# Moving a few small operations of routing and start-up between engines and steps

## The chip, the cores and the metric

One core of one Trainium2 chip runs the whole program. The metric is device time in microseconds (us), the median of the runs shown. The engines are named as the profile names them: PE (TensorE, matrix products) with PEld (its weight loads), DVE (VectorE), ACT (ScalarE), POOL (GpSimd) and SP (SyncE, which issues most of the DMAs).

## The reference

Attention in which a query sees only the keys of its own hash bucket, and behind it a layer of eight experts, each token going to the one with the highest logit:

```python
q_bits = (einsum('bhsd,dk->bhsk', q, proj) > 0)        # 6 bits, same for k
mask = q_bucket[:, :, :, None] == k_bucket[:, :, None, :]
scores = where(mask, scale * q @ k.T, -1e9)
attn = exp(scores - max(scores)); attn /= sum(attn) + 1e-9
x = (attn @ v) laid out as (B*S, H*D)                  # 3072 tokens x 512
logits = x @ w_gate                                    # 8 experts
expert = argmax(logits); weight = softmax(logits)[expert]
out[token] = weight * (relu(x @ w1[expert]) @ w2[expert])
```

There are 4 batches, 8 heads, 768 positions and 64 channels a head; w1 is 512 x 1024 and w2 1024 x 512 for each expert.

## The kernel before

The attention goes through 16 pairs of heads (pr = 0 to 15, four to a batch), each in two groups of 384 queries (g = 0, 1), each group in six steps (n = 0 to 5) of 128 queries of one head: 192 steps. The order of PE, DVE, ACT and SP is that in which the program is written; POOL's order is left to a scheduler, except for instructions wrapped in `in_turn`, which keep the written order among themselves.

A step i issues the scores of step i + 2 (`scores`: two products for each of two column ranges, L234 and L235), the row maximum on DVE (L237) and the exponential of step i + 1 on ACT (L253). Then come a small piece of other work, the transposes of probabilities (L278) and, in every second step, 24 products with v (L296). The codes of the buckets are carried as extra rows of the second operand of the scores.

At the start there is no pair before to hide behind. `first_k` and `first_q` make the operands of the two heads of pair 0: a rounded part (q1, k1) by ACT or DVE, the rest by a subtraction (L200 on DVE for head 0 and on POOL for head 1, L226 on POOL for q of both heads), and the codes (L205, L227, weighed by L210). The first scores need all of these for head 0. Two copies that only the routing of tokens needs, the triangle `tri` and the start of the counts `run` (L548, L549), are issued on POOL in front of them in the program.

A batch is routed in two groups. The pieces of `route` are put on a list, `light`, from which a step takes one: the logits, their gathering, the one-hot choice, `ranks` (PE counts the tokens of each expert in front of a token, into a PSUM tile `rk` of the pool `ps_m`, which has one buffer named `misc`), and `rows` (slot and weight of each token, and the scatter of its row to DRAM by POOL, L395). `av_out` transposes finished outputs into another tile of the same one buffer (L326) and scales them (L327). For the first group of a batch `rows` takes the next piece of the list in the same step, and that is `av_out` of the second group.

After the third batch `pick_first` chooses the expert that is computed first (L607 to L620): the fullest one by the counts so far. Its weights and rows are fetched during the last pairs, its first products (L729) run while the last rows are still scattered, and the eight experts follow.

`early_logits` (L502 to L517) sums three of the four pairs of the last group ahead of its end, in the last group's steps 0 and 1. `last_route` treats the last 384 tokens in three chains of 128; its first piece, `evac`, copies the output out of PSUM (L432).

Of the kernel before, what the change touches and what calls it, by code (L numbers as in the profile page):

```python
# [8 lines left out]
F32 = mybir.dt.float32  # L9
# [4 lines left out]
ALU = mybir.AluOpType  # L14
AX = mybir.AxisListType
# [3 lines left out]
P = 128  # L19
# [5 lines left out]
E, F = 8, 1024  # L25
# [33 lines left out]
def lsh_attention_moe_kernel(ctx, tc, qkd, q2d, k2d, v, pjbd, wg, w1, w2, ident_in, tri_in, cols_in, eoff_in, ids_in, out):  # L59
# [21 lines left out]
    tri = const.tile([P, P], BF16, name="tri")  # L81
    ones = const.tile([P, P], BF16, name="ones")
    V.memset(ones, 1.0)
    tiny = const.tile([P, 1], F32, name="tiny")
    V.memset(tiny, 1e-9)
    run = const.tile([P, E], F32, name="run")

    att = ExitStack()
# [38 lines left out]
    def in_turn(ins):  # L127
        if not in_turn_over:
            tc.keep_in_program_order(ins)
# [203 lines left out]
    def route(b, g):  # L333
# [19 lines left out]
        at = {}  # L353
# [22 lines left out]
        def ranks():  # L376
            A.activation(ex, lg, AF.Exp, bias=0.0, scale=1.0)
            rk = ps_m.tile([P, 512], F32, name="misc")
            PE.matmul(out=rk[:, 0:3 * E], lhsT=ident, rhs=run.unsqueeze(1).broadcast_to([P, 3, E]), start=True, stop=False)
            PE.matmul(out=rk[:, 0:3 * E], lhsT=tri, rhs=ohb, start=False, stop=False)  # L380
            PE.matmul(out=rk[:, E:3 * E], lhsT=ones, rhs=ohb[:, 0:2], start=False, stop=False)
            PE.matmul(out=rk[:, 2 * E:3 * E], lhsT=ones, rhs=ohb[:, 0], start=False, stop=True)
            for jj in range(3):
                PE.matmul(out=rk[:, 3 * E:4 * E], lhsT=ones, rhs=ohb[:, jj], start=jj == 0, stop=jj == 2)
            V.tensor_tensor(out=pos, in0=rk[:, 0:3 * E].rearrange("p (j e) -> p j e", e=E), in1=ohb, op=ALU.mult)
            V.tensor_tensor(out=run, in0=rk[:, 3 * E:4 * E], in1=run, op=ALU.add)
            V.reduce_sum(out=mx[:, :, 1:2], in_=ex, axis=AX.X)

        def rows():
            x = xrows[(b, g)]  # L390
            V.reduce_max(out=slot, in_=pos, axis=AX.X)
            V.tensor_tensor(out=mx[:, :, 1:2], in0=mx[:, :, 1:2], in1=tiny.unsqueeze(1).broadcast_to([P, 3, 1]), op=ALU.add)
            V.reciprocal(out=x[:, :, :, SEG + 1], in_=mx[:, :, 1:2].broadcast_to([P, 3, NG]))
            for jj in range(3):
                ins = G.indirect_dma_start(out=xs, out_offset=bass.IndirectOffsetOnAxis(ap=slot[:, jj, :], axis=0),  # L395
                                           in_=x[:, jj].rearrange("p g w -> p (g w)"), in_offset=None)
                rows_apart("xs", ins)
                if jj == 0 and b + 1 < B:
                    in_turn(ins)
            if not g and b + 1 < B:  # L400
                light.pop(0)()

        def pause():
            pass

        return [logits, gather_heads, one_hot, pause, ranks, rows] if b + 1 < B else [logits, gather_heads, one_hot, ranks, rows]

    def last_route(sums, o):
# [9 lines left out]
        def chain(jj, pools):  # L418
# [10 lines left out]
                return cell["t"]  # L429

            def evac():
                V.tensor_copy(out=ot, in_=o[:, js])  # L432
                G.tensor_scalar(out=sums[:, 2 * jj:2 * jj + 2], in0=sums[:, 2 * jj:2 * jj + 2], scalar1=1e-9, scalar2=None, op0=ALU.add)
                V.reciprocal(out=inv[:, jj], in_=sums[:, 2 * jj:2 * jj + 2])

# [109 lines left out]
    SY.dma_start(out=lsb[:, 0:P], in_=tri_in)  # L545
    SY.dma_start(out=eoff, in_=eoff_in)
    SY.dma_start(out=ids, in_=ids_in)
    G.tensor_copy(out=tri, in_=lsb[:, 0:P])  # L548
    G.tensor_copy(out=run, in_=eoff[:, 1])  # L549
    for hh in range(2):  # L550
        q1, k1 = (opp.tile([P, S], F32R, name=n) for n in ("q1", "k1"))
        operands[0][0][hh] += [q1, seconds(0)[:, 2 * hh], k1, seconds(0)[:, 2 * hh + 1]]
# [52 lines left out]
    def keys():  # L605

        V.tensor_tensor(out=key, in0=run, in1=eoff[:, 1], op=ALU.subtract)  # L607
        V.scalar_tensor_tensor(out=key, in0=key, scalar=float(2 * E), in1=eoff[:, 0], op0=ALU.mult, op1=ALU.add)

    def pick_first():  # L610

        def most():
            keys()
            V.reduce_max(out=best[:, 0:1], in_=key, axis=AX.X)

        def which():
            V.tensor_scalar(out=mark[:, 0], in0=key, scalar1=best[:, 0:1], scalar2=None, op0=ALU.is_equal)
            V.tensor_tensor(out=mark[:, 1], in0=mark[:, 0], in1=eoff[:, 0], op=ALU.mult)
            V.reduce_sum(out=best[:, 1:2], in_=mark[:, 1], axis=AX.X)
            V.tensor_scalar(out=best_i, in0=best[:, 1:2], scalar1=-1.0, scalar2=float(E), op0=ALU.mult, op1=ALU.add)  # L620

        return [most, which]

    def number(tile_1):
        return nc.values_load(tile_1, engines=[SY.engine], min_val=0, max_val=E - 1, skip_runtime_bounds_check_because=why)
# [115 lines left out]
    def out_and_route(pr, g):  # L741
        while divide:
            divide.pop(0)()
        if pr % NPAIR < NPAIR - 1:
            av_out(pr, g)
            return

        pieces = route(pr // NPAIR, g)
        pieces[0]()
        light.append(lambda: av_out(pr, g))  # L750
        light.extend(pieces[1:])
        if (pr, g) == (NPR - NPAIR - 1, 1):
            light.extend(pick_first())

    in_order.enter_context(tc.manual_schedule(engines={PE.engine, V.engine, A.engine, SY.engine}))
    put, weigh = first_k(0, V)
# [13 lines left out]
    for i, (pr, g, jj, hh) in enumerate(steps):  # L770
# [37 lines left out]
            run_expo(i + 1)  # L808
        if i == 0:
            weigh()  # L810
        while late:
            late.pop(0)()
        sums = sums_of(pr, g)
# [3 lines left out]
        side = (g, n) == (0, 2) and 0 < pr < NPR - 1  # L817
        if due and due[0][0] == i and not last:
            due.pop(0)[1]()
        elif light and not side and not last:  # L820
            light.pop(0)()
        if not last:
            for f, x in PREPARE[min(pr, 1)].get((g, n), ()) if pr + 1 < NPR else ():
# [19 lines left out]
            prev = (pr, g, sums)  # L843

        if last:
            if n < 2 and light:
                light.pop(0)()
            if n == 1:
                due.pop(0)[1]()
                while light:  # L850
# [400 lines left out]
```

## Time and profile before

| what | value |
|---|---|
| median of 3 runs | 727.81 us (725.92 to 729.55) |
| the profiled execution | 725.06 us |
| its span in the trace | 722.8 us, so 2.26 us lie around it |
| PE busy | 694.4 us (96%) |
| PEld, DVE, ACT, POOL busy | 85%, 72%, 64%, 57% |

Matrix products are pipelined and overlap, so busy PE is not PE at its peak. A stretch in which PE is not busy is of more use here: it is time in which it had nothing that could start. Attention ends at about 440 us; behind that PE is busy for the whole of nearly every stretch.

### The profile page before, as it was taken

The numbers are of one execution on the slowest core, as the hardware profiler recorded it, in microseconds if no ns is written. First come the engines' busy times: TensorE is split into PE (matmuls) and PEld (weight loads), VectorE is DVE, ScalarE is ACT, GpSimd is POOL, SyncE is SP. The second block draws the span as 40 slices with busy tenths as digits, with TensorE's granted clock in tenths as the row PEclk, the third lists the DMA queues.
The fourth block names the chain that finished last, engine by engine and source line by source line (L and its number), as shares of the span: only waits on it lengthen the run. The fifth ranks groups of instructions, "written<-read, shape, count | busy, mean of one in ns | idle before, by whom it ended". The sixth has DMA issues, their size and how long they took to land.

```text
span 722.8 us, 16061 instructions
## 1 busy us (share of the span) xinstructions
PE 694.4 (96%) x5735; PEld 612.1 (85%) x5735; DVE 517.1 (72%) x1018; ACT 463.8 (64%) x995; POOL 410.6 (57%) x405
## 2 busy tenths in 40 slices
PE   3999999999999999999989999999999999999995
PEld 1688888888887788887868879999999999999994
DVE  3857887888888988888998867656565657575641
ACT  3879888888888888897777853524242434354330
POOL 2577664776766586566766523018383838446461
PEclk9999999999999999999999999999999999999998
DMA  8788888889888989997987423765746465757521
GB/s 278 211 245 247 250 266 260 244 258 308 264 251 246 279 248 280 284 271 207 290 260 196 142 58 109 198 169 145 185 130 195 128 194 163 201 167 222 156 70 46
DMA packets 110081, 150.33 MB, mean 208 GB/s; under 512 B 12548, under 2 KB 77990, under 8 KB 109992
## 3 DMA queue, kind: packets, MB, share of 16 engines
q1 hardware_dynamic: 105016, 136.52, 65.2%
q0 software_dynamic: 4976, 12.69, 4.9%
q8 instruction: 47, 0.77, 0.5%
q14 instruction: 42, 0.34, 0.1%
HBM read 94.23 MB, written 55.18 MB: 207 GB/s over the span
## 4 chain that ended last, share of the span: by engine, by line
issue 21%; POOL 14%; PE 11%; DVE 3%; DMA 3%; ACT 1%; SPq 1%; POOLq 1%; ACTq 0%; DVEq 0%
POOL y L1026 11%; PE o L296 4%; PE s L234 2%; PE t L278 2%; POOL yo L1024 2%; DMA y<-yo,tok 2%; PE s L235 1%; DVE m L237 1%; DMA xr<-xs 1%; ACT p L253 1%; PE s L729 1%; DMA xs<-xr,slot 0%; POOL tags L947 0%; PE misc L326 0%; POOL tags L943 0%
## 5 line engine op out<-in xcount | busy, mean ns | idle before, releaser
L237 DVE TENSOR_REDUCE m<-s 128x1 f32<-128x768 f32 x192 | 182.4, 950 | 56.3 <-PE s L235 41.3
L234 PE MATMUL s<-k,q 128*128 128x512 f32 (+1 forms) x384 | 149.2, 388 | 15.3 <-POOL q L226 7.4
L296 PE MATMUL o<-pt,vt 128*64 128x128 f32 x2304 | 146.8, 277 | 0.0
L296 PEld LDWEIGHTS o<-pt,vt 128*64 128x64 f32 x2304 | 123.8, 137 | 16.9 <-issue 10.8
L235 PE MATMUL s<-c 76*128 76x512 f32 (+1 forms) x384 | 123.6, 343 | 0.1
L253 ACT ACTIVATE p<-s,m 128x768 f32<-128x768 f32 x111 | 110.2, 993 | 16.2 <-DVE m L241 12.5
L281 ACT COPY pt<-t 128x384 f32<-128x384 f32 x222 | 95.6, 485 | 39.0 <-PE t L278 37.1
L1026 POOL DMA_INDIRECT y<-yo,tags x88 | 103.5, 1176 | 24.9 <-issue 22.6
L234 PEld LDWEIGHTS s<-k,q 128*128 128x128 f32 x384 | 73.2, 191 | 48.0 <-ACT pd L253 10.1
L278 PE MATMUL t<-ident,p 128*128 128x128 f32 x666 | 92.3, 274 | 0.0
L984 ACT ACTIVATE hh<-hps 128x352 fp32r<-128x352 f32 (+3 forms) x56 | 27.9, 499 | 96.8 <-PE hps L998 96.8
L698 DVE TENSOR_TENSOR wlo<-wraw,whi 128x1024 fp32r<-128x1024 f32 x60 | 73.3, 1223 | 18.2 <-ACT whi L693 18.2
L278 PEld LDWEIGHTS t<-ident,p 128*128 128x128 f32 x666 | 75.0, 140 | 11.0 <-issue 9.4
L253 ACT ACTIVATE pd<-s,m 128x768 f32<-128x768 f32 x81 | 80.2, 991 | 5.0 <-DVE m L241 0.7
L269 DVE STREAM_TRANSPOSE pt<-pq 128x768 f32<-128x768 f32 x81 | 78.4, 968 | 6.0 <-DMA pq<-moved 6.0
L235 PEld LDWEIGHTS s<-c 76*128 76x128 f32 x384 | 73.9, 193 | 9.0 <-ACT c L210 0.4
L1017 PE MATMUL hps<-hh,wlo 128*128 128x436 f32 (+6 forms) x224 | 75.8, 339 | 0.0
L1017 PE MATMUL hps<-hh,whi 128*128 128x448 f32 (+9 forms) x224 | 75.8, 338 | 0.0
L1017 PE MATMUL hps<-hl,whi 128*128 128x436 f32 (+6 forms) x224 | 75.7, 338 | 0.0
L998 PE MATMUL hps<-xh,whi 128*128 128x352 f32 (+3 forms) x224 | 75.3, 336 | 0.0
L998 PE MATMUL hps<-xl,whi 128*128 128x428 f32 (+6 forms) x224 | 74.9, 334 | 0.0
L998 PE MATMUL hps<-xh,wlo 128*128 128x428 f32 (+6 forms) x224 | 74.9, 334 | 0.0
(221 smaller groups left out, 1185.6 us busy)
## 6 DMA issues: line engine op xcount, KB each, us to landing
wraw<-w SPq DMA_DIRECT2D x64, 512.0 KB, 3.7
moved<-pd SPq DMA_DIRECT2D x324, 96.0 KB, 3.7
pq<-moved SPq DMA_DIRECT2D x81, 384.0 KB, 4.3
qk<-qkd SPq DMA_DIRECT2D x30, 384.0 KB, 8.7
xs<-zrow SPq DMA_DIRECT2D x8, 910.0 KB
vt<-v SPq DMA_DIRECT2D x16, 384.0 KB, 3.5
coded<-cr SPq DMA_DIRECT2D x15, 192.0 KB, 2.3
c<-coded SPq DMA_DIRECT2D x30, 72.0 KB
```

What stands on the lines that cost most here:

```text
L234: PE.matmul(out=s[:, c0:c1], lhsT=q1[:, qs], rhs=k1[:, c0:c1], start=True, stop=False)
L235: PE.matmul(out=s[:, c0:c1], lhsT=q2[0:KM, qs], rhs=k2[0:KM, c0:c1], start=False, stop=True)
L237: V.tensor_reduce(out=m[:, 0:1], in_=s[:, 0:S], axis=AX.X, op=ALU.max, negate=True)
L253: A.activation(to, of, AF.Exp, bias=m[:, 2:3], scale=m[:, 1:2], accum_out=sums[:, idx:idx + 1])
L269: V.transpose(out=pt()[:, hh].rearrange("p c (s j) -> p c s j", j=SQ), in_=q.rearrange("p s c i -> p c s i"))
L278: PE.transpose(out=t[:, i * P:i * P + P], in_=p[:, kc * P:kc * P + P], identity=ident)
L281: A.copy(out=dst, in_=src)
L296: PE.matmul(out=o[hh * D:hh * D + D, jj * P:jj * P + P], lhsT=vt[:, kc, hh * D:hh * D + D], rhs=pt[:, hh, kc], start=kc == 0, stop=kc == N ...
L698: loeng.tensor_tensor(out=lo[:, i:i + step], in0=cell["t"], in1=bf(hi[:, i:i + step]), op=ALU.subtract)
L998: PE.matmul(out=hps[:, 0:w], lhsT=wt[:, c, fs], rhs=xt[:, c, 0:w], start=n == 0, stop=n == 3 * NDC - 1)
L1017: PE.matmul(out=yps[:, 0:w], lhsT=wt[:, f, ds], rhs=ht[:, 0:w], start=n == 0, stop=n == 3 * NFC - 1)
L1026: rows_apart("out", G.indirect_dma_start(out=out_seg, out_offset=bass.IndirectOffsetOnAxis(ap=tags[:, i, 0:1].bitcast(I32), axis=0), in_=y ...
```

## The change

- `tri` and `run` are copied by POOL in step 0 behind the weighing of the codes, in written order with the other marked POOL work.
- `pick_first` takes over the last piece `rows` of the third batch's second group and returns seven pieces in place of two: the counts (three POOL operations in place of two DVE ones), `rows`, three empty steps, the maximum on DVE with two POOL operations behind it, and the sum and the conversion on DVE.
- The sum of exponentials (`reduce_sum` of `ex`) is written into three unused columns of `rk` in PSUM, and 1e-9 is added to it in `rows` by a `tensor_scalar` that reads PSUM. Before, the sum went to SBUF and a tile `tiny` was added by a `tensor_tensor`. The tile goes.
- The output of the third chain of `last_route` is copied by ACT, not DVE.
- The pieces of `early_logits` are taken in the last group's steps 0 and 1 right behind the scores, not behind the products with v.

```diff
             V.tensor_tensor(out=run, in0=rk[:, 3 * E:4 * E], in1=run, op=ALU.add)
-            V.reduce_sum(out=mx[:, :, 1:2], in_=ex, axis=AX.X)
+            at["ex"] = rk[:, 4 * E:4 * E + 3].unsqueeze(2)
+            V.reduce_sum(out=at["ex"], in_=ex, axis=AX.X)
 
         def rows():
             x = xrows[(b, g)]
             V.reduce_max(out=slot, in_=pos, axis=AX.X)
-            V.tensor_tensor(out=mx[:, :, 1:2], in0=mx[:, :, 1:2], in1=tiny.unsqueeze(1).broadcast_to([P, 3, 1]), op=ALU.add)
+            V.tensor_scalar(out=mx[:, :, 1:2], in0=at["ex"], scalar1=1e-9, scalar2=None, op0=ALU.add)
...
             def evac():
-                V.tensor_copy(out=ot, in_=o[:, js])
+                if jj == 2:
+                    A.copy(out=ot, in_=o[:, js])
+                else:
+                    V.tensor_copy(out=ot, in_=o[:, js])
...
-    G.tensor_copy(out=tri, in_=lsb[:, 0:P])
-    G.tensor_copy(out=run, in_=eoff[:, 1])
...
-    def pick_first():
+    def pick_first(rows):
+
+        def counts():
+            in_turn(G.tensor_tensor(out=key, in0=run, in1=eoff[:, 1], op=ALU.subtract))
+            in_turn(G.tensor_scalar(out=key, in0=key, scalar1=float(2 * E), scalar2=None, op0=ALU.mult))
+            in_turn(G.tensor_tensor(out=key, in0=key, in1=eoff[:, 0], op=ALU.add))
 
         def most():
-            keys()
             V.reduce_max(out=best[:, 0:1], in_=key, axis=AX.X)
+            in_turn(G.tensor_scalar(out=mark[:, 0], in0=key, scalar1=best[:, 0:1], scalar2=None, op0=ALU.is_equal))
+            in_turn(G.tensor_tensor(out=mark[:, 1], in0=mark[:, 0], in1=eoff[:, 0], op=ALU.mult))
 
         def which():
-            V.tensor_scalar(out=mark[:, 0], in0=key, scalar1=best[:, 0:1], scalar2=None, op0=ALU.is_equal)
-            V.tensor_tensor(out=mark[:, 1], in0=mark[:, 0], in1=eoff[:, 0], op=ALU.mult)
             V.reduce_sum(out=best[:, 1:2], in_=mark[:, 1], axis=AX.X)
...
-        return [most, which]
+        return [counts, rows, pause, pause, pause, most, which]
...
-            light.extend(pick_first())
+            light.extend(pick_first(light.pop()))
...
             weigh()
+            in_turn(G.tensor_copy(out=tri, in_=lsb[:, 0:P]))
+            in_turn(G.tensor_copy(out=run, in_=eoff[:, 1]))
...
-        elif light and not side and not last:
+        elif light and not side and (not last or n < 2):
             light.pop(0)()
...
-            if n < 2 and light:
-                light.pop(0)()
```

The order of the instructions shows three places. First POOL's first operations, of before and of the change. q_159 and q_162 are the q operands of heads 0 and 1 before, q_155 and q_158 the same two in the change; k and c belong to head 1.

```order
L200 ISA
L200 TENSOR_TENSOR c_161<-kr,k_163 64x768
L226 TENSOR_TENSOR q_162<-qr,q_162 64x384
L548 CAST tri<-lsb 128x128
L549 COPY run<-eoff 128x8
L226 TENSOR_TENSOR q_159<-qr,q_159 64x384
```

```order
L224 ISA
L224 TENSOR_TENSOR q_155<-qr,q_155 64x384
L198 TENSOR_TENSOR c_157<-kr,k_159 64x768
L224 TENSOR_TENSOR q_158<-qr,q_158 64x384
L815 CAST tri<-lsb 128x128
L816 COPY run<-eoff 128x8
```

The subtraction for q of head 0, which stood fifth among the operations, now stands first, and the two copies stand behind all three subtractions.

Second, DVE around `ranks` and `rows` of the first group of the first batch, of before and of the change; the first operation is the one that reads the ranks, and the last one scales what `av_out` of the second group transposes.

```order
L385 TENSOR_TENSOR pos<-misc,ohb 128x24
L386 TENSOR_TENSOR run<-misc,run 128x8
L387 TENSOR_REDUCE mx<-ex 128x3
L237 TENSOR_REDUCE m<-s 128x1
L238 TENSOR_SCALAR m<-m 128x1
L391 TENSOR_REDUCE slot<-pos 128x3
L392 TENSOR_TENSOR mx<-mx,tiny 128x3
L393 RECIPROCAL xr<-mx 128x12
L327 TENSOR_TENSOR xr<-misc,inv 128x3x128
```

```order
L383 TENSOR_TENSOR pos<-misc,ohb 128x24
L384 TENSOR_TENSOR run<-misc,run 128x8
L386 TENSOR_REDUCE misc<-ex 128x3
L235 TENSOR_REDUCE m<-s 128x1
L236 TENSOR_SCALAR m<-m 128x1
L390 TENSOR_REDUCE slot<-pos 128x3
L391 TENSOR_SCALAR mx<-misc 128x3
L392 RECIPROCAL xr<-mx 128x12
L325 TENSOR_TENSOR xr<-misc,inv 128x3x128
```

Nothing changes its place, but the last reading of the ranks' tile in `misc` is no longer the second row but the seventh, behind the next step's row maximum.

Third, PE in steps 0 and 1 of the last group, of before and of the change, between the scores of step 2 and the transposes of outputs.

```order
L278 MATMUL t<-ident,p 128x128 x6
L296 MATMUL o<-pt,vt 64x128 x24
L502 MATMUL misc<-ot,wg_sb 32x384 x3
L234 MATMUL s<-k_5746,q_5777 128x512
L235 MATMUL s<-c_5675 128x512
L234 MATMUL s<-k_5746,q_5777 128x256
L235 MATMUL s<-c_5675 128x256
L278 MATMUL t<-ident,p 128x128 x6
L296 MATMUL o<-pt,vt 64x128 x12
L508 MATMUL misc<-ident,lsb 128x96 x3
L326 MATMUL misc<-ident,ot 128x128 x3
```

```order
L501 MATMUL misc<-ot,wg_sb 32x384 x3
L276 MATMUL t<-ident,p 128x128 x6
L294 MATMUL o<-pt,vt 64x128 x24
L232 MATMUL s<-k_5745,q_5776 128x512
L233 MATMUL s<-c_5674 128x512
L232 MATMUL s<-k_5745,q_5776 128x256
L233 MATMUL s<-c_5674 128x256
L507 MATMUL misc<-ident,lsb 128x96 x3
L276 MATMUL t<-ident,p 128x128 x6
L294 MATMUL o<-pt,vt 64x128 x12
L324 MATMUL misc<-ident,ot 128x128 x3
```

The three products of the logits and the three transposes that gather them moved ahead of the transposes and products of their steps.

## Rows read from the trace of the kernel before

**Rows 1.** Windows: length, busy time by engine (instructions), clock, DMA share, GB/s.

```profile
250.00:300.00 50.00, 49.80 (x516) 42.01 (x512) 42.61 (x80) 44.79 (x107) 34.16 (x34) 1.00 0.92 278
...
600.00:650.00 50.00, 50.00 (x320) 50.00 (x320) 33.55 (x50) 22.96 (x36) 27.60 (x30) 1.00 0.64 185
```

**Rows 2.** Timeline of the start: start, duration, engine, line, operation, [idle before <-releaser].

```profile
5.02 0.51 ACT L224 CAST q<-qr 128x384 fp32r<-128x384 f32 x1 [2.79 <-DMA qr<-q2d]
...
6.37 1.18 ACT L210 ACTIVATE c<-c 12x384 fp32r<-12x384 f32 x2 [0.42 <-DVE c L205]
...
7.02 0.61 DVE L227 TENSOR_SCALAR c<-misc,cols 12x384 fp32r<-12x384 f32 x1
...
8.48 1.79 POOL L200 TENSOR_TENSOR c<-kr,k 64x768 fp32r<-64x768 f32 x1 [8.04 <-ACT k L197]
...
12.40 0.29 POOL L548 CAST tri<-lsb 128x128 bf16<-128x128 f32 x1 [1.06 <-DMA lsb<-tri]
...
12.91 0.99 POOL L226 TENSOR_TENSOR q<-qr,q 64x384 fp32r<-64x384 f32 x1
...
13.95 0.80 PE L234 MATMUL s<-k,q 128*128 128x512 f32 x1 [7.42 <-POOL q L226]
...
14.54 0.63 PE L235 MATMUL s<-c 76*128 76x512 f32 x1
```

**Rows 3.** A window of the start, the codes' way out, and the first scores of pair 1.

```profile
18.00:20.00 2.00, 2.00 (x14) 1.47 (x11) 1.87 (x5) 1.76 (x6) 0.00 (x0) 1.00 1.08 338
...
25.01 0.34 SPq L177 DMA_DIRECT2D coded<-cr  x1
...
41.34 0.40 PE L235 MATMUL s<-c 76*128 76x512 f32 x1
```

**Rows 4.** Timeline of the choice of the first expert, and its first line much later.

```profile
360.62 1.83 POOL L163 TENSOR_TENSOR q<-qk,q 64x768 fp32r<-64x768 f32 x1
...
360.86 1.62 DVE L607 TENSOR_TENSOR key<-run,eoff 128x8 f32<-128x8 f32 x1
...
362.51 0.73 DVE L608 SCALAR_TENSOR_TENSOR key<-key,eoff 128x8 f32<-128x8 f32 x1
...
365.27 0.74 DVE L617 TENSOR_SCALAR mark<-key,best 128x8 f32<-128x8 f32 x1
...
366.05 0.73 DVE L618 TENSOR_TENSOR mark<-mark,eoff 128x8 f32<-128x8 f32 x1
...
444.45 0.17 DVE L607 TENSOR_TENSOR key<-run,eoff 128x8 f32<-128x8 f32 x1
```

**Rows 5.** Windows behind the second batch's last ranks and behind the third's.

```profile
257.00:274.00 17.00, 16.80 (x166) 14.45 (x165) 14.62 (x26) 15.49 (x39) 15.44 (x16) 1.00 0.89 272
357.60:374.00 16.40, 13.09 (x126) 10.99 (x126) 14.98 (x28) 11.53 (x29) 12.29 (x14) 1.00 0.85 232
```

**Rows 6.** Timeline of the first batch's first group, from the ranks to the next maximum.

```profile
139.06 0.16 DVE L386 TENSOR_TENSOR run<-misc,run 128x8 f32<-128x8 f32 x1
...
139.37 0.52 PE L326 MATMUL misc<-ident,ot 128*128 128x128 f32 x3
...
139.54 0.96 DVE L237 TENSOR_REDUCE m<-s 128x1 f32<-128x768 f32 x1 [0.23 <-PE s L235]
...
140.69 0.15 DVE L392 TENSOR_TENSOR mx<-mx,tiny 128x3 f32<-128x3 f32 x1
...
142.32 0.92 DVE L237 TENSOR_REDUCE m<-s 128x1 f32<-128x768 f32 x1
```

**Rows 7.** The window behind it.

```profile
139.30:152.80 13.50, 13.23 (x132) 10.72 (x131) 12.61 (x33) 10.71 (x27) 6.82 (x7) 1.00 0.95 305
```

**Rows 8.** Timeline of step 1 of the last group.

```profile
425.62 0.56 DVE L305 COPY ot<-o 128x384 f32<-128x384 f32 x1 [0.66 <-PE o L296]
...
426.73 0.52 PE L326 MATMUL misc<-ident,ot 128*128 128x128 f32 x3 [0.76 <-DVE lw L510]
```

**Rows 9.** Timeline of the third chain's first copy.

```profile
439.26 0.29 DVE L432 COPY ot<-o 128x128 f32<-128x128 f32 x1 [0.31 <-PE o L296]
```

More of the change, by code (lines that the diff above doesn't have):

```diff
@@ L83, in lsh_attention_moe_kernel @@
     V.memset(ones, 1.0)
-    tiny = const.tile([P, 1], F32, name="tiny")
-    V.memset(tiny, 1e-9)
     run = const.tile([P, E], F32, name="run")
@@ L401, in rows @@
                 light.pop(0)()
-        def pause():
-            pass
         return [logits, gather_heads, one_hot, pause, ranks, rows] if b + 1 < B else [logits, gather_heads, one_hot, ranks, rows]
@@ L608, in keys, with pause @@
         V.scalar_tensor_tensor(out=key, in0=key, scalar=float(2 * E), in1=eoff[:, 0], op0=ALU.mult, op1=ALU.add)
-    def pick_first():
+    def pick_first(rows):
[3 more added lines that the diff above has]
+            in_turn(G.tensor_tensor(out=key, in0=key, in1=eoff[:, 0], op=ALU.add))
         def most():
-            keys()
             V.reduce_max(out=best[:, 0:1], in_=key, axis=AX.X)
+            in_turn(G.tensor_scalar(out=mark[:, 0], in0=key, scalar1=best[:, 0:1], scalar2=None, op0=ALU.is_equal))
+            in_turn(G.tensor_tensor(out=mark[:, 1], in0=mark[:, 0], in1=eoff[:, 0], op=ALU.mult))
         def which():
-            V.tensor_scalar(out=mark[:, 0], in0=key, scalar1=best[:, 0:1], scalar2=None, op0=ALU.is_equal)
-            V.tensor_tensor(out=mark[:, 1], in0=mark[:, 0], in1=eoff[:, 0], op=ALU.mult)
             V.reduce_sum(out=best[:, 1:2], in_=mark[:, 1], axis=AX.X)
             V.tensor_scalar(out=best_i, in0=best[:, 1:2], scalar1=-1.0, scalar2=float(E), op0=ALU.mult, op1=ALU.add)
-        return [most, which]
+        return [counts, rows, pause, pause, pause, most, which]
+    def pause():
+        pass
     def number(tile_1):
```

## The prediction

> **What bounds the kernel now.** I read the windows first, then the timeline wherever PE loses time. In a quiet stretch of attention PE is busy 49.80 of 50 us, in a stretch of the experts 50.00 of 50 [rows 1]. So PE sets the end: an edit counts by the time for which PE waits because of it. In the two stretches DVE is busy 42.61 and 33.55 us, so a DVE operation costs only where PE waits for DVE. Three places have to be looked at: the start, where PE waits 7.42 us for POOL [rows 2], the choice of the first expert, where PE is busy 13.09 of 16.40 us [rows 5], and the routing, where it is busy 13.23 of 13.50 us and any new wait lands on the path [rows 7].
>
> **The start.** The first scores wait for q of head 0. Its subtraction is the last of five POOL operations: it starts at 12.91 behind the copy of `tri`, which itself waited for its DMA until 12.40, and behind the subtraction of head 1, which could not start before 8.48 [rows 2]. In the change it stands first on POOL. Its input is ready when ACT ends at 5.02 + 0.51 = 5.53, so it runs from about 5.6 to 6.6. The first score product can go at about 6.7 rather than 13.95. The second needs the codes, whose last piece is done by ACT at 6.37 + 1.18 = 7.55 and by DVE at 7.02 + 0.61 = 7.63; it goes at about 7.7 rather than 14.54. That is 6.8 us. The operations that are put behind are not late: head 1's subtraction still starts at 8.48, because it waits for ACT, and both heads' operands are done by 11.4, while the scores of head 1 come fourth; `tri` and `run` are first read by the routing at 139 us. The upper bound is the first product's own move, 13.95 - 6.7 = 7.3. The lower bound is from POOL itself: before 8.48 the trace shows it doing nothing but four fills, so I can't see that it is able to start at 5.6. If it is ready only at 8.48, q ends at 9.5, the first product goes at 9.55, and 4.4 us are gained. I take 6.8, since POOL's 8.04 us of idleness end 0.08 us after ACT's copy did (the row names it as the releaser).
>
> One rule speaks against this. An instruction that loads POOL's program library stands in front of the first subtraction in both orders. The Trainium skill, GPSIMD Engine Reference, section Instruction dispatch, says that the first call of freshly loaded code pays about 6 us that no row of a profile shows. No row here shows such a load: the first operation took 1.79 us, and whether 6 us lay in its idle time can't be seen. Counted from the start of the program at about 0.7, POOL would be ready at an estimated 6.7, q would end at 7.7, and the gain would be some 6.2 us and not 6.8.
>
> **The routing.** The sum of exponentials now stays in the ranks' tile until `rows` reads it. The pool has one buffer, so the next tile in it, which `av_out` transposes into, has to wait for that reading. Before, the last reading ends at 139.06 + 0.16 = 139.22, and PE's transposes go at 139.37, without a stall. In the change the last reading is where L392 stands now: it ends at 140.69 + 0.15 = 140.84, because the next row maximum, 139.54 to 140.50, is ahead of it on DVE [rows 6]. PE's queue is in order: the transposes, and behind them 24 products and the next scores, move by 140.84 - 139.22 = 1.6 us. The maximum of those scores starts at 142.32, as soon as they are there, so DVE has no backlog that would give the time back. PE is idle for only 0.27 us of the 13.5 us that follow [rows 7]. This happens where `rows` and `av_out` fall into one step: the first groups of three batches. The second groups have two steps or more between, and the fourth batch a tile of another pool or nothing behind it. 3 x 1.6 = 4.8 us at most; at least nothing, if the wait is covered in a way I don't see. I take 4.6, near the upper end, because the rows show no cover. The new form of the addition itself saves nothing here: L392 takes 0.15 us as it is.
>
> **The choice of the first expert.** Four tiny DVE operations take 1.62, 0.73, 0.74 and 0.73 us, together 3.8; the first of them takes 0.17 us when POOL is idle, and here it ends when POOL's long subtraction does, at 360.62 + 1.83 = 362.45 [rows 4]. They delay the maxima, and PE is idle for 16.40 - 13.09 = 3.31 us, against 17.00 - 16.80 = 0.20 in the same stretch of the batch before [rows 5]. In the change five POOL operations do this work. DVE keeps a maximum, a sum and a conversion of some 0.16 us each in two later steps. The POOL operations of 8 columns stand behind the pair's operands, the last of which ends before the scatters, and behind them POOL has nothing urgent; the scatters of this group move by a step, and what they write is read more than 30 us later. So 3.1 us of PE time come back; 2.6 if the three remaining operations all show, 3.8 if all four long ones were on the path.
>
> **The small ones.** In step 1 of the last group PE's transposes go at 426.73, though DVE's copy ends at 425.62 + 0.56 = 426.18: they waited for the gathered logits to leave the one buffer [rows 8]. With the gathering ahead of the products this wait is gone, but the gathering's own third of a microsecond now delays the copy; 0.2 us remain, from nothing to 0.55. In the third chain ACT copies instead of DVE, whose copy is 0.29 us [rows 9]; DVE goes on with the other two chains. I take 0.1, from -0.1 to 0.3.
>
> **Sum.** 6.8 - 4.6 + 3.1 + 0.2 + 0.1 = 5.6 us. The profiled execution took 725.06 us (span 722.8 and 2.26 around it), so the change's would take 719.5. The median of the runs shown is 2.75 above that execution; on it the forecast is 727.8 - 5.6 = 722.2.
>
> **Rivals.**
> - POOL is not ready early: q starts at 8.48. For it: no real POOL operation is seen before. Against: the releaser in that row. The gain falls by 2.4 to 3.2 us: 724.6.
> - The new wait of the transposes is covered. For it: nothing but that DVE and ACT have some idle time in rows 7. Against: PE's own 0.27. Without the 4.6 the gain is 10.2: 717.6.
> - The early start is given back to DMA, and the change is slower. At 18 to 20 us the DMA engines are full (share 1.08) with the clearing of rows, and the codes of pair 1 go out at 25.01 when they have drained [rows 3]. In the change the codes would go out at about 18.2, behind the clearing, and two more clearings follow in the same queue before the codes are read back. If pair 1's codes come later than the scores ask for them, at 41.34 - 6.8 = 34.5, PE waits. When they come only as late as in before, all 6.8 us are lost, and the stall of the routing outweighs the choice: 4.6 - 3.1 - 0.3 = 1.2 us slower, 729.0. Against it: from 18.2 to 34.5 are 16 us for a small transfer each way. By the Trainium skill (DMA: Bandwidth & Descriptors, section Queues, rings and completion order) each DMA engine takes a queue's descriptors in their order, which would make the codes wait for the clearing; no run here shows it yet.
>
> **How the numbers follow.** The forecast gets 0.62, the late POOL 0.15, the covered wait 0.13, DMA 0.10. The bounds of the terms alone run from a gain of 2.0 (4.4 - 4.8 + 2.6 - 0.1, rounded down) to one of about 11. The forecast's own range is 719 to 724.5. For 8 in 10 with the other cases, and some for the runs' own spread of 1.8 us to either side, I take 716.5 to 726. A gain or loss of 0.5% is 3.6 us, about what can be told from no change. Faster by more: nearly all of the forecast, all of the covered wait, a little of the late POOL, 0.73. Within: most of the late POOL and of DMA, 0.22. Slower by more: 0.05, from DMA with some other loss on top.
>
> **What would show it.** The first score product of the changed kernel at 6.7 to 7.8 us rather than 13.95, with POOL's first subtraction at about 5.6, and everything up to 120 us earlier by the same 6.8: if that shrinks between 20 and 50 us, DMA took it. PE waiting about 1.6 us for DVE in front of the transposes of outputs, three times, some 100 us apart: if it is missing, my 4.6 is wrong. PE busy all but about 0.3 us where it lost 3.3 behind the third batch. What would make the forecast wrong is above all the size of the first two terms, which have opposite signs and of which neither operation has been seen in its new place.

## The result and the profile after

Four runs of each kernel on one chip: before 727.52 us (725.92 to 729.55), after 719.48 us (718.73 to 720.76), ratio 0.989 with an interval of 0.986 to 0.992. The forecast was 722.2 us in a range of 716.5 to 726.0, so the time fell where it was expected. The profiled execution of the changed kernel took 720.76 us, span 718.5, where the sum gave 719.5.

The same two kernels were compared twice more in the experiments, on chips on which the kernel before took 735.01 and 732.69 us, with twelve runs of the changed kernel each, and there the change was worth nothing: 0.998 and 1.001. So there are two things to explain: why the sum fitted in the first comparison, and why it didn't in the later ones. Ratios leave out single executions that ran clearly slower than the others of their kernel, and where the profiled execution of a version was one of these, its windows are not given.

The start, in the timeline of the changed kernel (start, duration, engine, line, operation, idle before and its releaser), against [rows 2, 3]:

```profile
5.34 0.51 ACT L222 CAST q<-qr 128x384 fp32r<-128x384 f32 x1 [3.11 <-DMA qr<-q2d]
...
5.94 0.99 POOL L224 TENSOR_TENSOR q<-qr,q 64x384 fp32r<-64x384 f32 x1 [5.50 <-ACT q L222]
...
6.98 0.79 PE L232 MATMUL s<-k,q 128*128 128x512 f32 x1
...
8.31 0.77 PE L233 MATMUL s<-c 76*128 76x512 f32 x1 [0.54 <-DVE c L225]
...
18.82 0.34 SPq L175 DMA_DIRECT2D coded<-cr  x1
...
35.24 0.40 PE L233 MATMUL s<-c 76*128 76x512 f32 x1
```

POOL's subtraction starts 0.09 us after ACT's copy ends (5.34 + 0.51 = 5.85). The second product goes at 8.31, not 14.54: 6.2 us. The codes of pair 1 go out at 18.82 and the scores that read them run at 35.24, 6.1 us earlier than before, so DMA took next to nothing back.

The routing. First the waits of PE (engine, line, tile, releaser: total us, times, longest), then the timeline around the first two of them, answering to [rows 6]:

```profile
PE misc L324 <- DVE mx L391: 4.5, 3, 1.5
```

```profile
134.51 0.74 PE L324 MATMUL misc<-ident,ot 128*128 128x128 f32 x3 [1.49 <-DVE mx L391]
135.19 2.83 PE L294 MATMUL o<-pt,vt 128*64 128x128 f32 x24
...
239.16 0.52 PE L324 MATMUL misc<-ident,ot 128*128 128x128 f32 x3 [1.49 <-DVE mx L391]
239.61 1.53 PE L294 MATMUL o<-pt,vt 128*64 128x128 f32 x24
...
242.09 0.96 DVE L235 TENSOR_REDUCE m<-s 128x1 f32<-128x768 f32 x1 [0.93 <-PE s L233]
...
422.23 0.55 PE L324 MATMUL misc<-ident,ot 128*128 128x128 f32 x3
434.88 0.27 ACT L429 COPY ot<-o 128x128 f32<-128x128 f32 x1
```

The three waits are there, 1.49 us each (two are shown). Behind the first one 24 products take 2.83 us and not 1.53. Further down are the two small edits: the transposes at 422.23 no longer wait (0.76 us in [rows 8]), and ACT's copy takes 0.27 us where DVE's took 0.29 [rows 9].

To see what a stretch costs I measure from one preparation of codes on POOL (L151 before, L149 after, fifteen in the program) to the next. Two such windows of before: the first routing, and the choice of the first expert (length, busy time by engine, granted clock, DMA share, GB/s):

```profile
125.55:152.83 27.28, 26.69 (x269) 21.81 (x268) 24.27 (x62) 22.18 (x54) 18.56 (x19) 1.00 0.88 267
354.85:384.10 29.25, 25.94 (x259) 21.52 (x257) 26.40 (x54) 21.72 (x50) 18.41 (x18) 1.00 0.85 249
```

The same windows of after, with one inside the first and that of the third routing:

```profile
119.10:149.56 30.46, 28.40 (x269) 23.02 (x268) 24.63 (x62) 22.18 (x54) 18.54 (x19) 0.94 0.81 235
134.70:138.00 3.30, 3.30 (x28) 2.64 (x26) 1.44 (x2) 0.96 (x2) 2.46 (x3) 0.50 0.94 310
326.03:354.91 28.88, 26.82 (x269) 21.77 (x268) 24.70 (x62) 22.17 (x54) 18.40 (x18) 1.00 0.85 253
354.91:381.09 26.18, 26.01 (x271) 22.10 (x271) 22.35 (x50) 21.61 (x50) 19.60 (x24) 1.00 0.87 268
```

The second and third routing cost 1.6 us each (28.87 and 28.88 against 27.27 and 27.25), as worked out. The first costs 3.2: right behind its wait the granted clock is 0.50 for 3.3 us, the lower of its two levels (1.2 GHz of 2.4), before it is 1.00 again. The choice gives back 29.25 - 26.18 = 3.07. From the last such point to the end it is 337.4 us after 338.7: 1.3 less. Start 6.2, routing -6.4, choice 3.1, end 1.3 and some 0.1 elsewhere make the 4.3 us by which the two profiled spans differ; the medians differ by 8.0, since the profiled run of after was the slowest of its four, and that of before (725.06) faster than all of its four.

### The profile page after: what moved, and what is told of

The parts are those of the page before. It is cut to its first block, busy times and chain, and to the rows that moved or that the text cites. A ratio compares the mean times of both kernels' runs of the same rounds, so it can differ in the third digit from the quotient of the medians.

```text
span 718.5 us, 16071 instructions
## 1 busy us (share of the span) xinstructions
PE 695.6 (97%) x5735; PEld 612.9 (85%) x5735; DVE 512.9 (71%) x1012; ACT 463.9 (65%) x996; POOL 411.6 (57%) x410
## 4 chain that ended last, share of the span: by engine, by line
issue 22%; POOL 14%; PE 11%; DMA 3%; DVE 2%; SPq 1%; ACT 1%; POOLq 1%
POOL y L1030 11%; PE o L294 4%; PE t L276 2%; PE s L232 2%; POOL yo L1028 2%; DMA y<-yo,tok 2%; PE s L233 2%; DMA xr<-xs 1%; DVE m L235 1%; PE s L733 1%; PE misc L324 0%; DMA xs<-xr,slot 0%; POOL tags L951 0%; ACT p L251 0%; POOL tags L947 0%
## 5 line engine op out<-in xcount | busy, mean ns | idle before, releaser
L294 PEld LDWEIGHTS o<-pt,vt 128*64 128x64 f32 x2304 | 124.9, 138 | 17.1 <-issue 11.0
L276 PEld LDWEIGHTS t<-ident,p 128*128 128x128 f32 x666 | 75.0, 141 | 11.8 <-issue 9.4
L1021 PE MATMUL hps<-hh,whi 128*128 128x448 f32 (+9 forms) x224 | 75.7, 338 | 0.0
L1021 PE MATMUL hps<-hl,whi 128*128 128x436 f32 (+6 forms) x224 | 75.6, 338 | 0.0
L1021 PE MATMUL hps<-hh,wlo 128*128 128x436 f32 (+6 forms) x224 | 75.6, 338 | 0.0
## 6 DMA issues: line engine op xcount, KB each, us to landing
qk<-qkd SPq DMA_DIRECT2D x30, 384.0 KB, 10.3
```

What stands on the lines that cost most here:

```text
L276: PE.transpose(out=t[:, i * P:i * P + P], in_=p[:, kc * P:kc * P + P], identity=ident)
L294: PE.matmul(out=o[hh * D:hh * D + D, jj * P:jj * P + P], lhsT=vt[:, kc, hh * D:hh * D + D], rhs=pt[:, hh, kc], start=kc == 0, stop=kc == N ...
L1021: PE.matmul(out=yps[:, 0:w], lhsT=wt[:, f, ds], rhs=ht[:, 0:w], start=n == 0, stop=n == 3 * NFC - 1)
```

## The experiments

Three groups of four kernels, each group on a chip of its own with runs of before beside it (medians 735.01, 734.46 and 732.69 us). Ratios are to before on the same chip. Windows are those between preparations of codes; "routing" is the mean of the three windows in which the change has its routing wait, "choice" that with the choice.

| version | runs | median us | ratio (interval) | routing | choice |
|---|---|---|---|---|---|
| change | 12 | 734.32 | 0.998 (0.995 to 1.001) | 31.2 | 26.3 |
| change, again | 12 | 734.57 | 1.001 (0.998 to 1.004) | 30.0 | 26.3 |
| change, sum in SBUF | 6 | 723.88 | 0.986 (0.982 to 0.989) | 27.3 | 26.4 |
| the same, again | 7 | 723.39 | 0.987 (0.984 to 0.990) | - | - |
| change, copies first | 9 | 739.97 | 1.008 (1.005 to 1.011) | 30.2 | 26.3 |
| change, old choice | 12 | 733.92 | 0.998 (0.996 to 1.000) | 29.7 | 26.8 |
| change, addition early | 12 | 728.07 | 0.994 (0.991 to 0.996) | 28.4 | 26.4 |
| the same, again | 6 | 727.60 | 0.992 (0.989 to 0.995) | 28.4 | 26.3 |
| before + sum in PSUM | 9 | 740.43 | 1.009 (1.005 to 1.013) | 30.0 | 26.8 |
| before + copies behind codes | 12 | 728.86 | 0.991 (0.988 to 0.994) | - | - |
| sum in SBUF, old choice | 12 | 728.06 | 0.993 (0.990 to 0.996) | 27.3 | 31.2 |
| sum in SBUF, choice spread on DVE | 7 | 725.21 | 0.991 (0.988 to 0.994) | 27.2 | 30.4 |

**The change itself, twice.**

> The changed kernel once more, as the yardstick for the others of this call. Expected 5.6 to 8 us below the kernel before on the same chip (the prediction's sum and the medians so far). In its trace the transposes of outputs wait about 1.5 us for DVE three times; where PE's granted clock falls behind one of these waits, as in the first trace of the change, another 1.4 us are lost there.

> The changed kernel once more, beside the versions below on one chip, since it stood at 0.989 of before in the first comparison and at 0.998 in the second. Theory (the routing wait costs 1.5 us three times, and from chip to chip up to 1.4 us more behind each; and the old choice of before pays for its collision or not): between these two, 0.989 to 0.998, and 0.010 to 0.014 above the version with the sum in SBUF. Rival (the second comparison was a disturbed chip): 0.987 to 0.991, and at most 0.007 above the version with the sum in SBUF.

It gained nothing on either chip. The start is as early as in the first comparison (the first preparation of codes at 17.1 and 16.6 us, there 17.5). What differs is the routing, and the stretch behind the last codes, to which the account of the prediction comes back. The second routing, in the timeline of the first of these two runs:

```profile
238.86 0.52 PE L324 MATMUL misc<-ident,ot 128*128 128x128 f32 x3 [1.48 <-DVE mx L391]
239.31 1.53 PE L294 MATMUL o<-pt,vt 128*64 128x128 f32 x24
...
241.91 0.82 PE L276 MATMUL t<-ident,p 128*128 128x128 f32 x6
...
242.88 0.96 DVE L235 TENSOR_REDUCE m<-s 128x1 f32<-128x768 f32 x1 [2.03 <-PE t L276]
...
243.66 0.86 ACT L279 COPY pt<-t 128x384 f32<-128x384 f32 x2 [3.66 <-PE s L233]
...
245.94 0.50 PE L232 MATMUL s<-k,q 128*128 128x512 f32 x1 [1.05 <-ACT pd L251]
```

The wait of 1.48 us is the same, and PE's products behind it are recorded at the same pace. But DVE's maximum starts 4.02 us after the transposes, where in the first comparison it was 2.93 (242.09 - 239.16). ACT's copy is late too: it starts 1.75 us after the transposes of probabilities that it reads (241.91), and 0.53 in the first comparison. The profile names PE as the releaser of both, so it looks as if PE's results came later than its rows, whose ends are modelled, let one think. And 7 us behind the first wait PE waits again, for an exponential that came late for that reason: 1.02, 1.05 and 1.39 us in the three routings. The first two windows are 30.0 - 27.3 = 2.7 us longer than before. In the third the granted clock falls as well, to its lower level; these are four microseconds behind the second wait:

```profile
356.00:360.00 4.00, 4.00 (x28) 3.33 (x26) 1.86 (x5) 1.65 (x6) 0.00 (x0) 0.50 0.71 194
```

That window, 33.6 us long, takes 3.6 more than the other two. Why the results were late at a granted clock of 1.00 is not in the records.

**The sum of exponentials back in SBUF.** One part undone: what the routing wait costs in all.

```diff
-            at["ex"] = rk[:, 4 * E:4 * E + 3].unsqueeze(2)
-            V.reduce_sum(out=at["ex"], in_=ex, axis=AX.X)
+            V.reduce_sum(out=mx[:, :, 1:2], in_=ex, axis=AX.X)
...
-            V.tensor_scalar(out=mx[:, :, 1:2], in0=at["ex"], scalar1=1e-9, scalar2=None, op0=ALU.add)
+            V.tensor_tensor(out=mx[:, :, 1:2], in0=mx[:, :, 1:2], in1=tiny.unsqueeze(1).broadcast_to([P, 3, 1]), op=ALU.add)
```

> The change without the sum of exponentials in PSUM: the sum goes to SBUF and the tile of 1e-9 is added, as before; all else as in the change. My theory: the three waits in front of the transposes go, and the kernel is 4.5 us faster than the change (up to 6 if a fallen clock goes with them). Rival: the waits are covered by work that is late anyway, and it takes the same time as the change within 1 us.

> The changed kernel with the sum of exponentials back in SBUF once more. Theory: no wait on misc, routing steps of 27.3 us, 0.982 to 0.988 of before again, the fastest of these four.

No wait on L326 is left in the routing. Its windows are as in the kernel before, and that of the choice as in the change (the first routing and the choice):

```profile
119.10:146.40 27.30, 26.71 (x269) 21.82 (x268) 24.27 (x62) 22.25 (x54) 18.62 (x19) 1.00 0.83 254
351.00:377.40 26.40, 25.25 (x257) 21.26 (x256) 22.30 (x50) 21.52 (x50) 19.68 (x24) 1.00 0.88 266
```

Against the changed kernel on the same chip this is 0.0125 and 0.0141 of some 734 us, 9.2 and 10.3 us: twice the 4.5 us that the waits themselves last, and more than the first expectation (4.5, up to 6) had. This version is the fastest of all that were run.

**The addition alone moved up.** The sum stays in PSUM; only its last reader comes earlier. If the single buffer is the cause, the wait goes.

```diff
             V.reduce_sum(out=at["ex"], in_=ex, axis=AX.X)
+            V.tensor_scalar(out=mx[:, :, 1:2], in0=at["ex"], scalar1=1e-9, scalar2=None, op0=ALU.add)
...
             V.reduce_max(out=slot, in_=pos, axis=AX.X)
-            V.tensor_scalar(out=mx[:, :, 1:2], in0=at["ex"], scalar1=1e-9, scalar2=None, op0=ALU.add)
```

> The changed kernel with one instruction moved: the add of 1e-9 to the sum of exponentials (which reads the PSUM buffer misc) stands in the step that makes the sum, right behind it, and no longer in the step after it. Theory one buffer (the products of av_out wait only because the add still has to read the one misc buffer): all three waits of 1.5 us on L324 go, with what followed them, and the kernel lands within 0.3% of the one with the sum in SBUF, ratio to before 0.983 to 0.989 where that one was 0.986; routing steps from one code preparation to the next of 27.3 us instead of 30. Rival (the sum in PSUM costs by itself, by the writes and reads of VectorE there): waits stay or the time stays near the changed kernel's, ratio 0.995 to 1.00.

> The changed kernel with the add of 1e-9 right behind the sum in PSUM, once more, beside the version with the sum in SBUF on one chip. Theory (what is left of the wait, 0.37 us instead of 1.49, still holds up the next steps: its routing steps took 28.5 us against 27.3): 3 to 6 us slower than the version with the sum in SBUF, 0.004 to 0.008 above its ratio, and 0.004 to 0.008 below the changed kernel's. Rival (they are the same and only the chips differed): within 0.002 of the version with the sum in SBUF.

The wait shrinks to 0.37 us, what the sum and the addition themselves take. In the timeline of the first of the two runs, and its window:

```profile
133.13 0.52 PE L324 MATMUL misc<-ident,ot 128*128 128x128 f32 x3 [0.37 <-DVE mx L387]
```

```profile
118.80:147.30 28.50, 26.95 (x269) 21.83 (x268) 24.47 (x62) 22.34 (x54) 18.59 (x19) 1.00 0.83 248
```

So the buffer is the cause. The first expectation (as fast as with the sum in SBUF) failed: even 0.37 us makes the window 1.2 us longer (28.43 against 27.26), again with a wait for a late exponential behind it. On one chip the version stands at 0.992 against 0.987 and 1.001, as the second expectation had it against the sum in SBUF (0.005 above), and a little further from the change (0.009 below) than that said.

**Before with the sum in PSUM, and nothing else.**

```diff
-            V.reduce_sum(out=mx[:, :, 1:2], in_=ex, axis=AX.X)
+            at["ex"] = rk[:, 4 * E:4 * E + 3].unsqueeze(2)
+            V.reduce_sum(out=at["ex"], in_=ex, axis=AX.X)
```

> The kernel before with one part of the change: the sum of exponentials goes to PSUM and the add of 1e-9 reads it there in the step after. Theory one buffer: three waits of 1.5 us of the products of av_out on the add, and on a chip like that of the first experiments a second wait of 1 to 1.4 us behind each: slower than before by 4.5 us without and 7.5 to 8.5 us with the second waits, ratio 1.006 to 1.012; a fall of the granted clock behind one of them would add 1.5 to 3.5 us. Rival (the wait was there before, hidden elsewhere): within 0.3% of before.

0.0091 of 734.46 is 6.7 us slower: this part alone undoes the start. Why it is less than the 9 to 10 us above has a likely reason two experiments further on.

**The copies, undone and alone.**

```diff
-            in_turn(G.tensor_copy(out=tri, in_=lsb[:, 0:P]))
-            in_turn(G.tensor_copy(out=run, in_=eoff[:, 1]))
...
     SY.dma_start(out=ids, in_=ids_in)
+    G.tensor_copy(out=tri, in_=lsb[:, 0:P])
+    G.tensor_copy(out=run, in_=eoff[:, 1])
```

> The change with the copies of the triangle and the counts issued where they were before, so that POOL does the subtraction for q of head 0 last again; all else as in the change. My theory: the first scores go at about 14 us, everything behind is 6.2 to 6.8 us later, and the kernel is that much slower than the change. Rival: DMA, which is full from 26 us on, gives most of the start back, and it is less than 3 us slower.

> The kernel before with one part of the change: the copies of triangle and counts stand behind the codes of the first pair on GpSimd's queue. Theory (the first scores waited for them): first score product at about 7 us instead of 14 and everything after it 6 us earlier, 5.5 to 7 us faster than before, ratio 0.990 to 0.993. Rival (the loads that run beside take it back): ratio 0.997 to 1.000.

Undone in the changed kernel, 1.0081 - 0.9981 = 0.010, 7.3 us; added alone to before (the reverse of this diff), 0.009, 6.6 us. With the copies first, PE waits 6.75 us for POOL's subtraction again, and the first preparation of codes is at 23.4 us, not 17.1. Predicted were 6.8.

**The choice, old form, beside the wait and without it.**

```diff
-        return [counts, rows, pause, pause, pause, most, which]
+        return [most, which]
```

(with the five operations on POOL put back on DVE as L607 to L620 of the kernel before)

> The change with the choice of the first expert as before, on DVE in two steps; all else as in the change. My theory: PE loses its 3.1 us behind the third batch again, and the kernel is 3 us slower than the change. Rival: the time is lost to DVE in another place, and it is within 1 us.

> The changed kernel with the sum of exponentials back in SBUF (no wait on misc) and the choice of the first expert as before: two steps on VectorE. Theory A (the old choice stalls because its first instruction meets GpSimd's work on the same rows, 1.62 us instead of 0.17, and seven operations stand in two steps; the stall was absent beside the routing wait only because the wait moved it clear of GpSimd): 2.5 to 3.5 us slower than the kernel with the sum in SBUF and the new choice, ratio to before 0.989 to 0.992 where that one had 0.986. Theory B (the choice never cost anything beside what the wait costs anyway on this chip): within 0.2% of that one, 0.984 to 0.988, and its step 26.4 to 26.9 us long.

Beside the routing wait the old form costs nothing: 0.998 either way, window 26.8 against 26.3 us. Without the wait it costs 31.24 - 26.37 = 4.9 us of window, and by ratio 0.9931 against 0.9856 on another chip, 5.5 us. Part of that is the granted clock, which is 0.50 from 367.3 to 374.0 us in this trace, from the second of two waits of PE of 1.63 and 1.24 us on; the same old form took 3.07 us more than the new one in the first comparison, where the clock stayed at 1.00. The timelines say why it stalls. The old form without the wait, DVE beside POOL:

```profile
358.79 1.82 POOL L163 TENSOR_TENSOR q<-qk,q 64x768 fp32r<-64x768 f32 x1
...
359.03 1.62 DVE L605 TENSOR_TENSOR key<-run,eoff 128x8 f32<-128x8 f32 x1
...
360.57 0.82 POOL L164 CAST c<-qk 64x768 fp32r<-64x768 f32 x1
...
360.68 0.73 DVE L606 SCALAR_TENSOR_TENSOR key<-key,eoff 128x8 f32<-128x8 f32 x1
```

Each DVE operation ends with the POOL operation that it met: 360.65 and 360.61, 361.41 and 361.39. The other two of the four, a step later, are held as well (0.75 and 0.73 us). Beside the wait, in the change with the old form, the first meets only the end of a POOL operation (364.42 + 0.82 = 365.24), and the second has just started when the long one goes:

```profile
364.42 0.82 POOL L160 CAST q<-qk 64x768 fp32r<-64x768 f32 x1
...
365.07 0.19 DVE L604 TENSOR_TENSOR key<-run,eoff 128x8 f32<-128x8 f32 x1
365.30 0.17 DVE L605 SCALAR_TENSOR_TENSOR key<-key,eoff 128x8 f32<-128x8 f32 x1
365.32 1.84 POOL L161 TENSOR_TENSOR q<-qk,q 64x768 fp32r<-64x768 f32 x1
```

Counted from the preparation of codes on POOL, the long operation starts after 5.8 us in both, but the choice after 5.5 us here (365.07 - 359.55) and after 6.0 there (359.03 - 353.0), as in the kernel before (360.86 - 354.85). The routing wait shifts the engines against each other by half a microsecond, and the start of the choice out of POOL's way; its last two operations are still held (0.32 and 0.84 us). In "before + sum in PSUM" the choice window is as short (26.8 us), so what that part lost to the wait it probably had partly back from the choice; before itself was not traced on that chip.

The Trainium skill, SBUF — State Buffer, section Who interferes with whom, says that a DVE instruction with two inputs in SBUF and a GpSimd instruction that reads SBUF exclude each other for a whole instruction, the one issued first going first, while a reduction is not held. The rows agree: 1.62 and 0.73 us against 0.19 and 0.17, and L611, a reduction beside POOL's 1.84 us at 365.50, took 0.16.

**Spread over the seven steps, but on DVE.** Is it the spreading or the engine?

```diff
-            in_turn(G.tensor_tensor(out=key, in0=run, in1=eoff[:, 1], op=ALU.subtract))
-            in_turn(G.tensor_scalar(out=key, in0=key, scalar1=float(2 * E), scalar2=None, op0=ALU.mult))
-            in_turn(G.tensor_tensor(out=key, in0=key, in1=eoff[:, 0], op=ALU.add))
+            keys()
...
-            in_turn(G.tensor_scalar(out=mark[:, 0], in0=key, scalar1=best[:, 0:1], scalar2=None, op0=ALU.is_equal))
-            in_turn(G.tensor_tensor(out=mark[:, 1], in0=mark[:, 0], in1=eoff[:, 0], op=ALU.mult))
+            V.tensor_scalar(out=mark[:, 0], in0=key, scalar1=best[:, 0:1], scalar2=None, op0=ALU.is_equal)
+            V.tensor_tensor(out=mark[:, 1], in0=mark[:, 0], in1=eoff[:, 0], op=ALU.mult)
```

> The changed kernel with the sum in SBUF and the choice of the first expert in the same seven steps, its five operations on the rows of experts on VectorE again and not on GpSimd. Theory spread (what stalled was seven operations in two steps, with the collision of the first of them): within 0.002 of the version with the sum in SBUF, the step with the choice 26.4 to 27.0 us. Rival engine (the collision of VectorE with GpSimd's work hits every operation wherever it stands): 0.003 to 0.007 above it, the step 29 to 31 us as in the kernel before and in the version with the old choice.

0.991 against 0.987 on one chip, 2.9 us, with overlapping intervals; the window, 30.4 against 26.4 us, is clear, and part of it is a fall of the granted clock (0.94 over the window, 0.50 from 375.2 to 378.4 behind a wait of PE of 1.96 us). Three of the four that had been held met POOL in their new steps too, the first for 0.74 us and two more as shown here:

```profile
368.83 1.81 POOL L172 TENSOR_TENSOR c<-qk,k 64x768 fp32r<-64x768 f32 x1
...
369.45 1.22 DVE L615 TENSOR_SCALAR mark<-key,best 128x8 f32<-128x8 f32 x1
...
370.69 0.82 POOL L173 CAST k<-qk 64x768 fp32r<-64x768 f32 x1
370.71 0.82 DVE L616 TENSOR_TENSOR mark<-mark,eoff 128x8 f32<-128x8 f32 x1
```

On POOL, in the version with the sum in SBUF, the five take 0.2 to 0.3 us each, and DVE's reduction 0.15:

```profile
363.03 0.21 POOL L611 TENSOR_TENSOR key<-run,eoff 128x8 f32<-128x8 f32 x1
363.32 0.24 POOL L612 TENSOR_SCALAR key<-key 128x8 f32<-128x8 f32 x1
363.65 0.20 POOL L613 TENSOR_TENSOR key<-key,eoff 128x8 f32<-128x8 f32 x1
...
368.26 0.15 DVE L616 TENSOR_REDUCE best<-key 128x1 f32<-128x8 f32 x1
...
368.51 0.32 POOL L617 TENSOR_SCALAR mark<-key,best 128x8 f32<-128x8 f32 x1 [0.59 <-DVE best L616]
368.91 0.21 POOL L618 TENSOR_TENSOR mark<-mark,eoff 128x8 f32<-128x8 f32 x1
```

So it is the engine that takes the stall away, and not the spreading: the operations stand in POOL's own queue and meet nobody.

The two small edits, the early logits and the last copy, were not run by themselves.

## Why the prediction was right, and where it was not

**The start: right.** 6.8 were forecast, 6.2 measured in the first comparison and 6.6 and 7.3 by the later ones. What is missing in the first comparison lies ahead of the change: ACT's copy started 0.32 us later than in [rows 2], and DVE's codes, for which the second product waited, 0.53. The rival of a late POOL fell: POOL started 0.09 us behind its input. So did the rival of DMA, by the codes of pair 1. By the Trainium skill (GPSIMD Engine Reference, section Instruction dispatch) POOL was to be ready at an estimated 6.7; its row has 5.94, and the measurement decides against that here. That the gain came out at the 6.2 us which this rule had given is a coincidence: the late codes made it.

**The routing wait: the mechanism right, the price too small.** The reasoning from one buffer, from DVE's order and from PE's queue held to 0.1 us: three waits of 1.49, none other, and moving the reader removes them. The term of 4.6 us is the time of the wait alone. Measured were 6.4 us in the first comparison, 8.3 and 11.8 in the windows of the two later traces of the change, and 9 to 10 by ratio. What failed is the step "3 x 1.6 = 4.8 us at most": it left out what follows an idle PE. In the first comparison the granted clock fell once, which cost 1.6 us; in the others late results of PE and a second wait came behind nearly every one, and a fall of the clock behind some.

The sentence that the new form of the addition saves nothing, as L392 takes 0.15 us, was read off one row. In before it takes 0.65 to 0.67 us in the second groups of the first three batches, because there it meets POOL as the choice does; the change's form, which reads PSUM, takes 0.15 us beside POOL. The first two rows are of before, the other two of after:

```profile
156.82 0.82 POOL L173 CAST k<-qk 64x768 fp32r<-64x768 f32 x1
...
156.99 0.67 DVE L392 TENSOR_TENSOR mx<-mx,tiny 128x3 f32<-128x3 f32 x1
```

```profile
153.54 0.82 POOL L171 CAST k<-qk 64x768 fp32r<-64x768 f32 x1
...
153.74 0.15 DVE L391 TENSOR_SCALAR mx<-misc 128x3 f32<-128x3 f32 x1
```

So the sum in PSUM gives DVE 1.5 us in all, against the 6 to 12 us that its wait costs PE.

**The choice: right where it was measured, but not a term by itself.** 3.07 came back in the first comparison for 3.1 forecast. Yet in the later comparisons the old form didn't stall beside the routing wait, so there the new form is worth 0.5 us of window in this change, and 5 us, a fall of the clock included, only without the wait. There the sum added two terms that exclude each other. Whether they did in the first comparison too stays open, as no version with one of them was run there; if they did, the 3.07 was met by luck.

**The small ones.** 0.3 forecast, and 1.3 measured behind the last codes, of which the wait of [rows 8] is 0.76; that the rest is theirs is not shown.

**The sum.** 5.6 us forecast; 4.3 between the profiled runs, 8.0 between the medians of the first comparison; 1.4 gained and 0.8 lost in the later ones (0.9981 and 1.0011). There the parts as measured (6.6 for the start, 5 for the choice without the wait, 9 to 10 lost to the wait) leave 1 to 2.5 us of gain, so the pieces close within their intervals. The time was met where the wait was cheap, and partly by luck: the start was 0.6 us and the wait 1.8 us worse than their terms, the end 1.0 better, and the rest of the way to 8.0 is the spread of the runs. With the prices of the later comparisons the forecast should have been "no change". One sum of the bounds is off as well: the best values of the terms (7.3, 0, 3.8, 0.55, 0.3) give a gain of 12 us, not of about 11.

That the later times are longer altogether has little to do with the change: from the last preparation of codes to the end it was 337.4 us in the first comparison and 342 to 348 in the ten later traces that have windows here, whatever the version. One such place is the last copy out of PSUM, for which PE waited 1.4 to 2.8 us in all ten and in neither trace of the first comparison; in nine of them the granted clock fell to 0.50 there for at least 3 us. It is so in the change, where ACT makes the copy, and in "before + sum in PSUM", where DVE does (waits of PE, one line of each kernel):

```profile
PE t L437 <- ACT ot L429: 2.2, 1, 2.2
```

```profile
PE t L437 <- DVE ot L431: 1.4, 1, 1.4
```

So the engine of that copy is not what decides it; what does stays open. A second place lies among the experts, where PE waits 0.9 to 1.2 us for weights that ACT prepares (L1021 in the change) in eight of the ten; the two without that wait, the first "addition early" and "choice spread on DVE", have the shortest ends, 343.0 and 341.8 us.

## What to carry to other kernels

A value that is left in a PSUM buffer keeps that buffer until its last reader has run; look which step that reader stands in, and what PE has queued for the same buffer. Where PE is the bound, count a new wait of PE at more than its length, here 1.4 to 2.6 times, and try the part alone and undone on more than one chip before adding terms up. Tiny operations on two tables in SBUF are not tiny on DVE while POOL is reading SBUF: put them where POOL runs them itself, or let one input come from PSUM.

## What the runs showed of the hardware

- A wait of PE of 1.5 us is in some cases followed by a granted clock of 0.50 (1.2 GHz of 2.4): of the 18 routing waits of 1.5 us in the traces of the change, "copies first", "old choice" and "before + sum in PSUM", it came right behind two, for 3.3 us (the first of the profiled run of after, the second of "change, again"), and in the third routing of the first later trace of the change behind a second wait, for 6.7 us. Behind the others it stayed at 1.00. At 0.50 the 24 products took 2.83 us for 1.53.
- In the later comparisons DVE's maximum behind such a wait started 0.4 to 1.8 us later than in the first (3.28 to 4.74 us behind the transposes, and 2.93), though PE's rows show the products at the same pace and the clock at 1.00. ACT's copy of the next transposes was 0.5 to 1.3 us late as well (1.00 to 1.79 us, and 0.53). Even a wait of 0.37 us was followed by a window 1.2 us longer. The cause is open, and so is what sets these comparisons apart from the first.
- A DVE operation of the kinds named here that starts while POOL runs a subtraction or a copy on SBUF ends 0.02 to 0.04 us after POOL's operation does: tensor_tensor, scalar_tensor_tensor and tensor_scalar on 8 columns in SBUF (1.62, 0.73 and 1.22 us), and the tensor_tensor on 3 columns (0.67). Reductions, the tensor_scalar of one column at 0.15 us and the one that reads PSUM at 0.15 us ran beside POOL.
